# Two more head pairs take their V rows straight from memory, and the attention phase gets a new list

## The chip, the cores and the metric

The kernel runs on one core of a Trainium2 chip. The metric is the device time of one execution in microseconds (us). The core has a matmul engine (PE, whose weight loads are listed apart as PEld), a vector engine (DVE), an activation engine (ACT), a general engine (POOL), and SP, which here only issues DMAs. Each engine works through its own instructions in order; a semaphore makes one wait for another.

## The reference

Three stages follow one another. Attention over 2 batches of 8 heads (768 positions of 64 elements) sees, for each query, a band of keys (|distance| < 16) together with 24 block summaries (the block maximum of K, the block mean of V):

```
k_sum = k.reshape(B, H, nb, 32, D).max(axis=3)
v_sum = v.reshape(B, H, nb, 32, D).mean(axis=3)
scores_l = where(|i - j| < 16, scale * q @ k.T, -1e9)
scores_s = scale * q @ k_sum.T + log(32)
a = softmax(concat([scores_l, scores_s]))
attn = a @ concat([v, v_sum])
```

A token mixer and a channel mixer follow (`u = x + (relu(x.T @ w_tok1) @ w_tok2).T`, then `u + relu(u @ w_ch1) @ w_ch2`), and a second channel mixer behind a layer norm (2048 hidden columns). Everything is fp32.

## The kernel before

Two heads make a pair: 8 pairs, i = 0 to 7, four for each batch. A pair's 768 positions are cut into 12 windows of 64, and four windows make one quad, so there are 24 quads, n = 0 to 23, three to a pair. For one quad the attention phase does this, each step by a letter and a number:

- `q` (PE): scores, 8 small matmuls; `m` (DVE): mask, scale and row minimum; `e` (ACT): exponential into `pr`; `t` (PE): four transposes of `pr`; `c` (ACT): copy of them to `PT`; `a` (PE): product with V, tile `av`; `n` (DVE): division by the row sums into `u`.
- For each pair: `l` loads K and Q, `k` (DVE) forms the block maxima, `K` (ACT) or `J` (POOL) copies them beside the keys.

V reaches its tile `V[i % 3]` (rows are keys, columns are the two heads' elements) in one of two ways. For pairs i < `NT` (4 before), `v` loads a transposed V with a border (tile `VW`, 552 KB); `s` (DVE) or `p` (POOL) sums its blocks, `S` (ACT) or `T` (POOL) writes their means into it, `w` (PE, L446) transposes four windows per call, and `x` (ACT) or `X` (DVE) copies the result out of PSUM (L453). That is three `w` and three copies for a pair. For pairs i >= `NT`, `r` loads the finished rows into `V` (780 KB, L354), `v` loads a transposed V without borders (tile `VT`, 384 KB) for the means alone, `s` (POOL, L400 and L403) folds its blocks in halves, `S` (PE, L426) transposes the sums (tile `psv`), `z` (ACT, L430) scales them, and `u` (POOL, L438) copies them to the V rows.

Between the quads stand pieces of the token mixer: `g` starts piece k on PE, `G` and `H` copy its result out (ACT and DVE). Pieces 0 to 3, 10, 11, 20 and 21 are its first product (L575, tile `g`), 4 to 9 its second for batch 0 (L317 to L319), 12 to 19 transposes of `u` (L620). `h`, `W`, `D`, `C` and `O` load, unpack and split weights; `f` is a filler matmul on a tile of zeros (L1194).

The order is written out by hand: the string `FRONT` is walked from left to right, and each engine gets its instructions in that order. Nothing is moved later. A wait in one entry so holds up all that stands behind it on the same engine, and on SP all loads behind it. When the list is through, the channel mixer begins with the first matmul of `g_('u', 0)_3`; from there on no list is involved.

PSUM tiles of `w` and of the mixer's pieces come from a pool of two banks (`ps_mm`); the filler has a tile of the same pool. `t` and `psv` share two banks of `ps_pt`. `P` starts a transposing piece in a bank of `ps_pt`.

Of the kernel before, what the change touches and what calls it, by code (L numbers as in the profile page):

```python
# [11 lines left out]
F32 = mybir.dt.float32  # L12
# [3 lines left out]
AF = mybir.ActivationFunctionType  # L16
# [13 lines left out]
NK = 96 + NB  # L30
# [14 lines left out]
EARLY = 16  # L45
NEG = -8e9
EPS = 1e-9
NT = 4
FRONT = """
d0 f d1 f j0 f f j1 f f i0 v0 f i1 f l1 f K0 f v1 q0 l2 f f m0 f f e0 f h1 q1 t0 m1 f c0 f q2  # L50
e1 f m2 f l3 e2 t1 s0 f f f v2 t2 k1 S0 h2 w1 v3 w0 K1 x1 h0 q3 X0 c1 w2 m3 p1 a0 e3 q4 n0 c2 t3 m4
x2 a1 e4 k2 q5 T1 a2 n1 K2 c3 w3 m5 W1 t4 x3 D1 q6 c4 a3 e5 n2 w5 m6 w4 x5 t5 x4 n3 q7 p2 c5 k3 a4
e6 m7 a5 e7 t6 n4 r4 q8 n5 J3 S2 p3 t7 c6 m8 h4 w7 W2 y2 w6 X7 c7 q9 l4 e8 X6 a7 D2 v4 a6 S3 W0 v5
n7 w11 l5 w9 m9 x11 t8 x9 w8 D0 c8 q10 x8 w10 n6 e9 g1 X10 W4 k4 D4 K4 s4 t9 m10 C4 g0 c9 O4 G1 e10
H1 s5 q11 G0 H0 t10 l6 m11 S4 a8 e11 k5 q12 h3 z4 t11 c10 h7 n8 u4 a9 h5 m12 v7 e12 a10 n9 r5 J5 q13
n10 c11 t12 m13 a11 c12 k6 e13 q14 S5 a12 J6 m14 z5 e14 u5 t13 n12 q15 n11 c13 t14 W3 m15 a13 W7 D3
q16 e15 g2 m16 e16 s7 n13 D7 C3 c14 t15 O3 C7 q17 c15 t16 m17 G2 a14 e17 H2 q18 n14 r7 c16 a15 m18
e18 a16 l7 n15 q19 n16 W5 g3 h6 D5 v6 h8 m19 C5 h9 e19 r6 O5 t17 t18 G3 c17 q20 H3 k7 c18 g7 m20 K7
e20 g5 H7 W6 q21 H5 s6 g8 m21 e21 D6 S7 g6 W8 H8 h10 C6 D8 z7 t19 W9 u7 S6 g4 z6 O6 h11 H6 u6 q22 H4
g9 m22 e22 q23 H9 a18 m23 b g19 n18 g12 G19 a17 G12 H19 t20 H12 c19 g13 n17 c20 g16 t21 G16 a19 G13  # L60
H16 e23 a20 H13 n19 g11 c21 n20 t23 G11 g15 H11 t22 G15 g14 c22 H15 a21 G14 g18 c23 n21 a22 G18 H14
a23 n22 g10 n23 H18 g20 G10 H10 g21 G20 H20 P17 G21 G17 H21 H17
"""
SCALE = 1.0 / math.sqrt(D)

# [1 line left out]
def f32(ap):  # L67
    return ap.bitcast(F32)


class Kern:
# [342 lines left out]
    def prep_v2(self, i):  # L414
        nc = self.nc
        if i < NT:
            zs = self.vs.pop(i)
            nc.scalar.activation(
                self.wide[i][:, :, 0:NB],
                zs.rearrange("p (o n) -> p o n", o=1).to_broadcast([P, 7, NB]),  # L420
                AF.Copy,
                scale=1.0 / BLOCK,
            )
            return
        self.psv = self.ps_pt.tile([P, 512], F32, tag="pt", name=f"psv{i}")
        nc.tensor.transpose(self.psv[:NK, 0:P], self.Z[i % 2], self.ident)  # L426

    def prep_v3(self, i):
        self.zs = self.att.tile([NK, P], F32, tag="zs", bufs=1, name=f"zs{i}")
        self.nc.scalar.activation(self.zs, self.psv[:NK, 0:P], AF.Copy, scale=1.0 / BLOCK)  # L430

    def prep_v4(self, i):
        nc, src = self.nc, self.zs
        V = self.V[i % 3].rearrange("p (w j) c -> p j w c", j=2)
        for a, j in ((0, 0), (96, 1)):
            out = V[a : a + NB, j, :, 0:130].rearrange("p w (r c) -> p w r c", r=2)[:, :, :, 0:64]
            x = src[a : a + NB].rearrange("p (o r c) -> p o r c", o=1, r=2).to_broadcast([NB, 6, 2, 64])
            nc.gpsimd.tensor_copy(out, x)  # L438

    def att_vtr(self, n):  # L440
        i, qd = divmod(n, 3)
        ps = self.ps_mm.tile([P, 512], F32, tag="mm", name=f"vtr{n}")
        for u in range(4):
            w = 4 * qd + u
            a = 184 * (w // 2) + 88 * (w % 2)
            self.nc.tensor.transpose(ps[:NK, u * P : u * P + P], self.flat_vt(i)[:, a : a + NK], self.ident)  # L446
        self.vps[n] = ps
# [748 lines left out]
    def run(self):  # L1196
        tc, nc, ctx = self.tc, self.nc, self.ctx
# [38 lines left out]
        self.vs, self.vps, self.sn = {}, {}, {}  # L1236
# [220 lines left out]
```

## Time and profile before

| | |
|---|---|
| time, median of 3 runs | 558.04 us (557.51 to 558.55) |
| the profiled execution | 557.49 us, of which the trace's span is 555.7 us |
| PE busy over the span | 548.7 us (99%) |
| PEld busy | 495.0 us (89%) |
| DVE, ACT, POOL busy | 405.1, 272.2, 36.6 us |
| attention phase (start to the first matmul of the channel mixer) | 0 to 91.28 us |
| the rest | 91.28 to 555.7 us |

A PE row's duration runs from a matmul's start to its modelled end and overlaps the next one; how long PE is taken by an operation is read from the distance between starts. POOL works only in the attention phase.

### The profile page before, as it was taken

The page shows a single profiled execution, that of the slowest core. Times are in us where ns is not written, and L with a number is a line of the kernel's source. Part 1 is how long each engine was busy: PE and PEld are TensorE (multiplying, and loading weights), DVE is VectorE, ACT ScalarE, POOL GpSimd, SP SyncE. Part 2 cuts the span into 40 slices and gives each one's busy share as a digit, 9 for nine tenths or more (in the row PEclk, how much of TensorE's full clock was granted, in tenths as well). Part 3 has the DMA queues.
Part 4 walks back from the last instruction along what each step waited for, and adds up shares of the span by engine and source line. Part 5 has one row for each costly group of instructions (what it writes and reads, how often), then busy time and mean ns, then how long its engine had stood idle before and what let it go on. Part 6 is the DMA issues. An engine that isn't in the chain of part 4 may idle for free.

```text
span 555.7 us, 10285 instructions
## 1 busy us (share of the span) xinstructions
PE 548.7 (99%) x3673; PEld 495.0 (89%) x3674; DVE 405.1 (73%) x977; ACT 272.2 (49%) x602; POOL 36.6 (7%) x76
## 2 busy tenths in 40 slices
PE   8999999999999999999999999999999999999997
PEld 4887789898998989989999988988989999999997
DVE  5989874648876887665579957888866776777771
ACT  5979663138755645454787325554422222334320
POOL 7454400000000000000000000000000000000000
PEclk9999999999999999999999999999999999999999
DMA  8876810435788779888656996898787897777455
GB/s 326 313 298 242 327 57 1 151 109 197 248 297 292 266 282 315 283 313 296 230 207 234 317 312 195 284 313 278 257 300 234 292 314 253 240 234 254 162 168 173
DMA packets 55651, 137.00 MB, mean 247 GB/s; under 512 B 5681, under 2 KB 13489, under 8 KB 55601
## 3 DMA queue, kind: packets, MB, share of 16 engines
q1 hardware_dynamic: 55600, 136.36, 71.6%
q8 instruction: 29, 0.48, 0.3%
q14 instruction: 22, 0.17, 0.1%
HBM read 101.73 MB, written 34.60 MB: 245 GB/s over the span
## 4 chain that ended last, share of the span: by engine, by line
PE 91%; ACT 3%; DVE 2%; DMA 2%; POOL 0%; issue 0%; SPq 0%; DVEq 0%; POOLq 0%; ACTq 0%
PE m L319 8%; PE m L318 8%; PE m L317 8%; PE acc_x L318 4%; PE acc_x L319 4%; PE acc_x L317 4%; PE g L575 3%; PE acc_y L319 2%; PE acc_y L318 2%; PE acc_y L317 2%; DMA V<-in_v_dram 2%; ACT pr L519 1%; PE av L547 1%; PE acc_m L319 1%; PE acc_m L318 1%; PE acc_m L317 1%
## 5 line engine op out<-in xcount | busy, mean ns | idle before, releaser
L317 PE MATMUL m<-slot,slot 128*128 128x384 f32 (+1 forms) x136 | 45.8, 337 | 0.0
L319 PE MATMUL m<-slot,slot 128*128 128x384 f32 (+1 forms) x136 | 45.4, 334 | 0.0
L318 PE MATMUL m<-slot,slot 128*128 128x384 f32 (+1 forms) x136 | 45.4, 334 | 0.0
L319 PE MATMUL acc_x<-slot,al 128*128 128x512 f32 x96 | 37.8, 394 | 0.0
L318 PE MATMUL acc_x<-slot,ah 128*128 128x512 f32 x96 | 37.8, 394 | 0.0
L317 PE MATMUL acc_x<-slot,ah 128*128 128x512 f32 x96 | 37.5, 391 | 0.0
L519 ACT ACTIVATE pr<-sn,mn 128x120 f32<-128x120 f32 x96 | 29.7, 389 | 6.6 <-DVE mn L504 6.6
L317 PEld LDWEIGHTS m<-slot,slot 128*128 128x128 f32 x136 | 25.6, 188 | 1.8
L318 PEld LDWEIGHTS m<-slot,slot 128*128 128x128 f32 x136 | 25.6, 188 | 1.6
L165 DVE SCALAR_TENSOR_TENSOR dec<-stage,dec 128x512 uint32<-128x512 uint32 x36 | 25.5, 708 | 0.7
L319 PEld LDWEIGHTS m<-slot,slot 128*128 128x128 f32 x136 | 25.5, 188 | 0.0
L142 ACT ACTIVATE dec<-stage 128x512 f32<-128x512 f32 x36 | 24.2, 676 | 0.1
L871 ACT ACTIVATE ah<-sm 128x384 fp32r<-128x384 f32 x16 | 8.4, 525 | 28.1 <-DVE sm L881 28.1
L575 PE MATMUL g<-u,tok 128*128 128x256 f32 x96 | 22.1, 383 | 0.0
L504 DVE CUSTOM_DVE_ANT_0 sn<-scores,mask 128x120 f32<-128x120 f32 x92 | 20.4, 277 | 2.2 <-PE scores L485 2.1
L703 ACT ACTIVATE f_B<-tx,gt 128x384 f32<-128x384 f32 x16 | 9.3, 582 | 25.4 <-PE tx L699 25.4
L319 PEld LDWEIGHTS acc_x<-slot,al 128*128 128x128 f32 x96 | 18.0, 188 | 4.0
L243 DVE TENSOR_TENSOR slot<-dec,slot 128x512 fp32r<-128x512 f32 x27 | 20.1, 743 | 0.1
L319 PE MATMUL acc_y<-slot,al_s 128*128 128x256 f32 x72 | 20.1, 280 | 0.0
L318 PE MATMUL acc_y<-slot,ah_s 128*128 128x256 f32 x72 | 20.1, 279 | 0.0
L575 PEld LDWEIGHTS g<-u,tok 128*128 128x128 f32 x96 | 17.8, 190 | 2.6 <-issue 0.3
L666 ACT ACTIVATE xn<-u,nb,rs 128x128 f32<-128x128 f32 x48 | 20.1, 483 | 0.0
(1516 smaller groups left out, 1732.5 us busy)
## 6 DMA issues: line engine op xcount, KB each, us to landing
stage<-in_wts_dram SPq DMA_DIRECT2D x62, 512.0 KB, 4.4
slot<-w1s SPq DMA_DIRECT2D x94, 256.0 KB, 3.6
w1s<-sps SPq DMA_DIRECT2D x16, 512.0 KB, 4.4
w2s<-sp SPq DMA_DIRECT2D x16, 512.0 KB, 3.4
slot<-w2s SPq DMA_DIRECT2D x16, 512.0 KB, 4.8
w2t<-wk SPq DMA_DIRECT2D x16, 512.0 KB, 5.0
slot<-w2t SPq DMA_DIRECT2D x8, 768.0 KB, 5.0
slot<-w2s SPq DMA_DIRECT2D x22, 256.0 KB, 4.3
```

The lines of the kernel that those rows point to most:

```text
L142: fold = lambda out: nc.scalar.activation(out, high, AF.Prelu, scale=2.0**-112, alpha=-(2.0**32))
L165: put(m, t[:, :, 0], 29, m, op0=ALU.logical_shift_right, op1=ALU.bitwise_or)
L243: (engine or nc.vector).tensor_tensor(wl, x, f32(wh), op=ALU.subtract)
L317: nc.tensor.matmul(out, lhs[0], rhs[0], start=first, stop=False)
L318: nc.tensor.matmul(out, lhs[0], rhs[1], start=False, stop=False)
L319: nc.tensor.matmul(out, lhs[1], rhs[0], start=False, stop=last)
L504: nc.vector.tensor_tensor_reduce(sn[:, u], ps[u % 2][:, u // 2, :NK], self.mask[:, mv], scale=-SCALE, scalar=3e38, op0=ALU.add, op1=ALU.mi ...
L519: self.nc.scalar.activation(self.pr[n][:, u], sn[:, u], AF.Exp, bias=mn[:, u : u + 1], scale=-1.0)
L575: nc.tensor.matmul(ps[:, :256], self.tok1(st, t), self.u[:, b * ST + st, 256 * hf : 256 * hf + 256], start=st == 0, stop=st == ST - 1,)
L666: nc.scalar.activation(xn[:, j], self.u[:, g * GT + j, cc * P : cc * P + P], AF.Identity, bias=nb[:, j : j + 1], scale=rs[:, j : j + 1],)
L703: nc.scalar.activation(x, ps[:, :GN], AF.Copy, scale=self.gt[:, cc : cc + 1])
L871: nc.scalar.activation(ah, x, AF.Relu)
```

## The change

`NT` falls from 4 to 2: pairs 2 and 3 take the way of pairs 4 to 7. The tiles that hold a pair's sums between `S`, `z` and `u` are kept by pair, so that two pairs can be under way at once. Two banks of `ps_mm` are taken as fixed tiles at the start, and a helper hands them out in turn; the filler writes to the first of them. `FRONT` is a new list. It has 16 fillers instead of 22, 6 `w` instead of 12, and 6 copies behind them instead of 12.

```diff
-NT = 4
+NT = 2
 FRONT = """
-d0 f d1 f j0 f f j1 f f i0 v0 f i1 f l1 f K0 f v1 q0 l2 f f m0 f f e0 f h1 q1 t0 m1 f c0 f q2
+d0 d1 f f j0 f j1 f v0 f l1 f i0 f v1 f i1 l2 f f K0 q0 v2 f h2 m0 q1 e0 f m1 f f e1 q2 t0 s0 l3 f
...
+    def mm_bank(self, name):
+        if not self.banks:
+            return self.ps_mm.tile([P, 512], F32, tag="mm", name=name)
+        self.banks.rotate(1)
+        return self.banks[0]
...
-        self.psv = self.ps_pt.tile([P, 512], F32, tag="pt", name=f"psv{i}")
-        nc.tensor.transpose(self.psv[:NK, 0:P], self.Z[i % 2], self.ident)
+        self.psv[i] = self.ps_pt.tile([P, 512], F32, tag="pt", name=f"psv{i}")
+        nc.tensor.transpose(self.psv[i][:NK, 0:P], self.Z[i % 2], self.ident)
...
     def att_vtr(self, n):
         i, qd = divmod(n, 3)
-        ps = self.ps_mm.tile([P, 512], F32, tag="mm", name=f"vtr{n}")
+        ps = self.mm_bank(f"vtr{n}")
...
     def g1(self, b, hf, t):
         nc = self.nc
-        ps = self.ps_mm.tile([P, 512], F32, tag="mm", name=f"g1_{b}_{hf}_{t}")
+        ps = self.mm_bank(f"g1_{b}_{hf}_{t}")
...
-            ps = self.bank or self.ps_mm.tile([P, 512], F32, tag="mm", name=f"tu_{g}_{cc}")
+            ps = self.bank or self.mm_bank(f"tu_{g}_{cc}")
...
-        self.wps = self.ps_mm.tile([P, 512], F32, tag="mm", name="warm_ps")
+        self.banks = deque(self.ps_mm.tile([P, 512], F32, tag="mm", name=f"mm{i}") for i in range(2))
+        self.wps = self.banks[0]
...
         with tc.manual_schedule(engines={E.PE}):
             self.attention()
+        self.banks = None
```

Counted over the two lists: `f` 22 to 16, `w` 12 to 6, `x` 8 to 4, `X` 4 to 2, `p` 3 to 1, `s` 5 to 7, `T` 1 to 2, `r` 4 to 6, `z` and `u` 4 to 6 each, `K` 5 to 7 and `J` 3 to 1; three splits of weights go from DVE (`O`) to POOL (`o`); three more transposing pieces stand in `ps_pt` banks (`P` 1 to 4). `S` falls from 7 to 6: of pairs 0 to 3 it had been an ACT copy for 0, 2 and 3, and is now a PE transpose for 2 and 3. All else in the list occurs as often as before. From the first matmul of the channel mixer on, the instructions of PE are the same in both programs.

PE, behind the third score product, up to the first transposes of V. Before:

```order
L485 MATMUL scores<-K_135,Q_132 64x120 x8
L1194 LDWEIGHTS warm
L1194 MATMUL warm_ps<-warm 128x512
...
L528 MATMUL pt_299<-ident,pr_279 120x128 x4
L1194 LDWEIGHTS warm
L1194 MATMUL warm_ps<-warm 128x512
...
L528 MATMUL pt_310<-ident,pr_294 120x128 x4
L446 MATMUL vtr_320<-ident,VW_109 120x128 x4
```

and now (line numbers are 6 higher from here on):

```order
L491 MATMUL scores<-K_133,Q_130 64x120 x8
L534 MATMUL pt_272<-ident,pr_245 120x128 x4
L1200 LDWEIGHTS warm
L1200 MATMUL mm_187<-warm 128x512
...
L534 MATMUL pt_284<-ident,pr_259 120x128 x4
L452 MATMUL mm_188<-ident,VW_109 120x128 x4
```

Behind the third score product there were two groups of transposes and five fillers before the first `vtr`, with one more group ahead of it; now there are two groups and two fillers in all. `mm_187` and `mm_188` are the two fixed banks.

PE, from the last transposes of probabilities before pair 2's V up to the first mixer piece. `VW_111` and `VW_112` are the transposed V of pairs 2 and 3. Before:

```order
L528 MATMUL pt_593<-ident,pr_559 120x128 x4
L446 MATMUL vtr_607<-ident,VW_111 120x128 x4
L446 MATMUL vtr_614<-ident,VW_111 120x128 x4
L485 MATMUL scores<-K_135,Q_132 64x120 x8
L547 MATMUL av_637<-V_142,PT_139 64x65 x8
L547 MATMUL av_649<-V_142,PT_138 64x65 x8
L446 MATMUL vtr_664<-ident,VW_112 120x128 x4
L446 MATMUL vtr_671<-ident,VW_112 120x128 x4
L528 MATMUL pt_683<-ident,pr_631 120x128 x4
L446 MATMUL vtr_689<-ident,VW_111 120x128 x4
L485 MATMUL scores<-K_135,Q_132 64x120 x8
L446 MATMUL vtr_706<-ident,VW_112 120x128 x4
```

and now:

```order
L432 MATMUL psv_553<-ident,Z_143 120x128
L534 MATMUL pt_555<-ident,pr_482 120x128 x4
L491 MATMUL scores<-K_133,Q_130 64x120 x8
L534 MATMUL pt_582<-ident,pr_540 120x128 x4
L553 MATMUL av_595<-V_139,PT_137 64x65 x8
L491 MATMUL scores<-K_133,Q_130 64x120 x8
L553 MATMUL av_625<-V_140,PT_136 64x65 x8
L534 MATMUL pt_639<-ident,pr_604 120x128 x4
L553 MATMUL av_655<-V_140,PT_137 64x65 x8
L491 MATMUL scores<-K_133,Q_130 64x120 x8
L534 MATMUL pt_677<-ident,pr_650 120x128 x4
L581 MATMUL mm_188<-u,tok 128x256 x6
```

Six groups of four transposes are gone, and one transpose of a pair's sums (`psv`) stands for three of them.

POOL, behind its work for pair 1. Before (`vh` are the halves of pairs 2 and 3, `VT_143` is the first pair that folds):

```order
L406 TENSOR_SCALAR VW_110<-vs_356 128x7x24
L376 TENSOR_TENSOR vh_521<-VW_111 128x384
...
L373 COPY K_135<-ks_528 128x7x24
L376 TENSOR_TENSOR vh_587<-VW_112 128x384
...
L376 TENSOR_TENSOR vs_586<-vh_587 128x24
L400 TENSOR_TENSOR VT_143<-VT_143 128x24x16
```

and now (`V_140` and `V_138` are the V tiles of pairs 2 and 3):

```order
L412 TENSOR_SCALAR VW_110<-vs_344 128x7x24
L406 TENSOR_TENSOR VT_141<-VT_141 128x24x16
...
L409 TENSOR_TENSOR Z_143<-VT_141 128x24 x2
L444 COPY V_140<-zs_574 24x6x2x64 x2
L406 TENSOR_TENSOR VT_142<-VT_142 128x24x16
...
L409 TENSOR_TENSOR Z_144<-VT_142 128x24 x2
L444 COPY V_138<-zs_733 24x6x2x64 x2
L243 TENSOR_TENSOR slot_103<-dec_674,slot_103 128x512
```

POOL now does the sums and the row copies of pairs 2 and 3 in turn, and a split of weights behind them.

## Rows read from the trace of the kernel before

**Rows 1.** Stretches: length, then busy time by engine, granted clock, DMA share, GB/s.

```profile
core 0: us, PE busy (x) PEld busy (x) DVE busy (x) ACT busy (x) POOL busy (x), PEclk, DMA share, GB/s
...
5.40:11.76 6.36, 6.22 (x72) 3.62 (x73) 4.00 (x26) 4.47 (x14) 3.94 (x6) 1.00 1.01 401
11.76:30.59 18.83, 18.60 (x329) 15.31 (x330) 17.30 (x84) 17.85 (x49) 8.61 (x20) 1.00 0.88 334
30.59:76.67 46.08, 44.05 (x571) 34.81 (x569) 41.90 (x173) 34.21 (x97) 19.69 (x34) 1.00 0.68 255
...
91.28:555.70 464.42, 461.18 (x2583) 427.17 (x2581) 333.82 (x674) 209.24 (x431) 0.00 (x0) 1.00 0.74 248
```

**Rows 2.** Waits of PE from 0 to 91.3 us: total, times, longest.

```profile
...
PE g L317 <- DVE u L604: 0.9, 1, 0.9
PE scores L485 <- POOL V L438: 0.5, 1, 0.5
PE scores L485 <- DVE mn L504: 0.4, 1, 0.4
```

**Rows 3.** Timeline of PE: start, duration, line, operation, count.

```profile
1.25 4.07 PE L1194 MATMUL warm_ps<-warm 128*128 128x512 bf16 x10 [1.25 <-DVE warm L1247]
...
5.98 1.25 PE L1194 MATMUL warm_ps<-warm 128*128 128x512 bf16 x5
...
10.37 0.81 PE L1194 MATMUL warm_ps<-warm 128*128 128x512 bf16 x3
11.02 0.66 PE L528 MATMUL pt<-ident,pr 128*120 128x128 f32 x4
11.76 1.09 PE L446 MATMUL vtr<-ident,VW 128*120 128x128 f32 x8
12.78 0.64 PE L485 MATMUL scores<-K,Q 64*64 64x120 f32 x16
...
39.59 1.15 PE L547 MATMUL av<-V,PT 121*64 121x65 f32 x32
...
43.01 0.33 PE L426 MATMUL psv<-ident,Z 128*120 128x128 f32 x1
43.27 0.69 PE L547 MATMUL av<-V,PT 121*64 121x65 f32 x16
...
91.28 0.42 PE L317 MATMUL g_('u', 0)_3_1578<-xt,slot 128*128 128x384 f32 x1
```

**Rows 4.** Groups of ACT up to 91.5 us: count, busy, mean ns, idle before.

```profile
...
L453 ACT COPY V<-vtr 120x512 f32<-120x512 f32 x8 | 4.5, 589 | 0.2 <-PE vtr L446 0.2
...
L373 ACT COPY K<-ks 128x168 f32<-128x168 f32 x5 | 1.7, 331 | 3.5 <-DVE ks L364 3.5
...
L430 ACT ACTIVATE zs<-psv 120x128 f32<-120x128 f32 x4 | 1.1, 264 | 1.6 <-POOL V L438 1.6
L418 ACT ACTIVATE VW<-vs 128x168 f32<-128x168 f32 x3 | 1.0, 338 | 0.1
```

**Rows 5.** Timeline of POOL.

```profile
19.78 1.02 POOL L376 TENSOR_TENSOR vh<-VW 128x384 f32<-128x384 f32 x1 [4.00 <-DMA VW<-in_vk_dram]
...
33.71 2.82 POOL L400 TENSOR_TENSOR VT<-VT 128x384 f32<-128x384 f32 x4 [7.90 <-DMA VT<-in_vt_dram]
...
49.73 2.47 POOL L438 COPY V<-zs 24x768 f32<-24x768 f32 x2 [6.04 <-DMA V<-in_v_dram]
...
65.86 2.06 POOL L438 COPY V<-zs 24x768 f32<-24x768 f32 x2 [0.27 <-ACT zs L430]
```

**Rows 6.** Timeline of DVE: one split beside POOL's work, one without.

```profile
34.12 1.14 DVE L243 TENSOR_TENSOR slot<-dec,slot 128x512 fp32r<-128x512 f32 x1
...
57.16 0.69 DVE L243 TENSOR_TENSOR slot<-dec,slot 128x512 fp32r<-128x512 f32 x1
```

**Rows 7.** Timeline of SP: the load of a weight half.

```profile
23.67 0.38 SPq L210 DMA_DIRECT2D stage<-in_wts_dram  x1
```

**Rows 8.** Tile V up to 95 us: times from issue to landing.

```profile
DMA to landing us min/median/max: 4.1/7.0/9.7
```

More of the change, by code (lines that the diff above doesn't have):

```diff
@@ L47 @@
 EPS = 1e-9
-NT = 4
+NT = 2
 FRONT = """
-d0 f d1 f j0 f f j1 f f i0 v0 f i1 f l1 f K0 f v1 q0 l2 f f m0 f f e0 f h1 q1 t0 m1 f c0 f q2
[L51 to L59, printed above, removed]
@@ L60 @@
-g9 m22 e22 q23 H9 a18 m23 b g19 n18 g12 G19 a17 G12 H19 t20 H12 c19 g13 n17 c20 g16 t21 G16 a19 G13
-H16 e23 a20 H13 n19 g11 c21 n20 t23 G11 g15 H11 t22 G15 g14 c22 H15 a21 G14 g18 c23 n21 a22 G18 H14
-a23 n22 g10 n23 H18 g20 G10 H10 g21 G20 H20 P17 G21 G17 H21 H17
+d0 d1 f f j0 f j1 f v0 f l1 f i0 f v1 f i1 l2 f f K0 q0 v2 f h2 m0 q1 e0 f m1 f f e1 q2 t0 s0 l3 f
+c0 f t1 m2 r2 e2 T0 h1 k1 w0 v3 w1 h0 K1 x0 q3 X1 c1 a0 m3 p1 e3 w2 n0 q4 x2 t2 m4 a1 e4 k2 q5 T1 t3
+m5 K2 s2 w3 c2 w5 e5 n1 q6 X5 a2 x3 m6 c3 t5 W2 n2 w4 e6 q7 k3 a3 m7 x4 t4 K3 D2 q8 c4 c5 a4 e7 m8
@@ new lines @@
+h4 S2 t6 r3 n4 q9 l4 z2 c6 u2 n3 t7 W1 m9 v4 a5 e8 D1 q10 s3 a6 c7 n5 W0 t8 m10 e9 a7 D0 q11 W4 v5
+t9 c8 h5 D4 g0 e10 l5 n6 h3 C4 m11 r4 e11 l6 n7 S3 g1 k4 z3 h7 G0 u3 H0 K4 c9 o4 q12 a8 m12 s5 a9
+e12 r5 n8 t11 t10 n9 G1 c11 q13 c10 a11 m13 s4 a10 e13 n11 q14 n10 W5 t12 t13 m14 g2 c13 H1 v6 c12
+k5 v7 l7 D5 K5 W3 S4 D3 C5 q15 h6 z4 g3 G2 u4 m15 e14 H2 C3 k6 o3 q16 G3 e15 a13 m16 o5 a12 e16 H3
+q17 n12 t14 m17 W7 S5 g8 c14 D7 K6 z5 e17 u5 t16 n13 t15 H8 g5 c15 s6 q18 a14 m18 a15 c16 r7 q19 n15
@@ L63 @@
+r6 s7 t17 h8 H5 g7 h9 c17 m19 e18 k7 g6 H7 S7 S6 H6 z7 q20 u7 t18 m20 g4 e20 n14 J7 z6 g9 e19 u6 W6
+q21 H9 a17 m21 a16 e21 H4 q22 c18 t19 m22 b g13 c19 t20 n17 W8 q23 n16 C7 a19 G13 D6 a18 g11 c20 H13
+h10 e22 m23 y2 n18 e23 n19 t21 G11 g15 c21 t22 H11 D8 G15 a20 C6 a21 c22 H15 h11 t23 n21 g14 c23 P16
+n20 a23 G16 G14 a22 n23 P12 n22 g10 G12 O6 W9 H12 H16 H14 P18 G10 g17 H10 P19 G17 g20 G19 H17 G18
+H18 g21 G20 H20 G21 H21 H19
 """
@@ L424, in prep_v2 @@
             return
-        self.psv = self.ps_pt.tile([P, 512], F32, tag="pt", name=f"psv{i}")
-        nc.tensor.transpose(self.psv[:NK, 0:P], self.Z[i % 2], self.ident)
+        self.psv[i] = self.ps_pt.tile([P, 512], F32, tag="pt", name=f"psv{i}")
+        nc.tensor.transpose(self.psv[i][:NK, 0:P], self.Z[i % 2], self.ident)
     def prep_v3(self, i):
-        self.zs = self.att.tile([NK, P], F32, tag="zs", bufs=1, name=f"zs{i}")
-        self.nc.scalar.activation(self.zs, self.psv[:NK, 0:P], AF.Copy, scale=1.0 / BLOCK)
+        self.zs[i] = self.att.tile([NK, P], F32, tag="zs", bufs=1, name=f"zs{i}")
+        self.nc.scalar.activation(self.zs[i], self.psv.pop(i)[:NK, 0:P], AF.Copy, scale=1.0 / BLOCK)
     def prep_v4(self, i):
-        nc, src = self.nc, self.zs
+        nc, src = self.nc, self.zs.pop(i)
         V = self.V[i % 3].rearrange("p (w j) c -> p j w c", j=2)
@@ L592, in g2 @@
         for st in range(ST) if only is None else (only,):
-            ps = self.ps_mm.tile([P, 512], F32, tag="mm", name=f"g2_{b}_{st}")
+            ps = self.mm_bank(f"g2_{b}_{st}")
             for t in range(2):
@@ L1235, in run @@
         self.VT = [att.tile([P, S], F32, name=f"VT{i}") for i in range(2)]
-        self.vs, self.vps, self.sn = {}, {}, {}
+        self.vs, self.vps, self.sn, self.psv, self.zs = {}, {}, {}, {}, {}
         self.Z = [att.tile([P, NK], F32, name=f"Z{i}") for i in range(2)]
```

## Prediction

> **What bounds the kernel now.** I first split the span at 91.28 us, where the channel mixer starts [rows 3]. Behind it PE works 461.18 of 464.42 us [rows 1], and the change leaves PE's instructions there as they are. So this part is carried along by whatever moves its start, and only the attention phase is open. A gain there is a gain in the total, unless a wait takes it.
>
> In the attention phase I read the stretches by engine next. From 11.76 to 30.59 us PE is busy 18.60 of 18.83 us, ACT 17.85 and DVE 17.30; from 30.59 to 76.67 us PE 44.05 of 46.08, DVE 41.90, ACT 34.21 [rows 1]. Nothing has much room before 30 us; later ACT has. Then I asked what PE waits for: the waits above 0.3 us, behind the first matmul, come to 0.9 + 0.5 + 0.4 = 1.8 us [rows 2]. A busy PE row may still hide a wait, since its end is modelled. So I take PE's costs from the distance between starts in the timeline [rows 3]: eight transposes of V take 12.78 - 11.76 = 1.02 us, 0.128 us each, and the next operation follows at once. Reading: PE sets the pace of the phase, with ACT and DVE close behind until 30 us.
>
> By the Trainium skill, page "Trainium Kernel Development and Optimization", section "Performance Expectations", busy matmul time says little about how full PE is, and the busy share of weight loads says more. PEld is at 15.31 of 18.83 us before 30.59 us [rows 1], so by that rule a fifth of this stretch is not PE's own, and work taken from PE there need not come back in full; this is the second rival below.
>
> **The change, part by part.** All in us on PE's path unless said otherwise.
>
> 1. *Six groups of four V transposes go* (pairs 2 and 3). 24 x 0.128 = 3.1. I take -3.0, since groups with other work on both sides come out a little shorter. Bounds: nothing, if PE waits for something else at these places; and -3.3, with a tenth more for the switch between shapes.
>
> 2. *Two transposes of block sums come.* One takes 43.27 - 43.01 = 0.26 [rows 3]: with 0.2 each, as it costs less between other 128-row transposes, +0.4. Bounds +0.2 to +0.6.
>
> 3. *Six fillers go.* Three take 11.02 - 10.37 = 0.65, so 0.22 each [rows 3], 1.3 for six. All stand in the first 12 us, where PE waits for the chain of scores, minimum and exponential: if this chain is no earlier, PE waits where it had filled, and the gain is 0. But the new list also puts the second quad's minimum and exponential straight behind the first's, where a copy out of PSUM had stood between them, and it starts V's transposes behind two groups of probabilities instead of three. So I take the full -1.3. Bounds 0 to -1.8.
>
> 4. *ACT.* Four copies out of PSUM (589 ns) and three of means (338 ns) go, two `zs` (264 ns) and two K copies (331 ns) come [rows 4]: -2.4 - 1.0 + 0.5 + 0.7 = -2.2 of ACT's time. DVE loses two copies and three splits, 0.69 to 1.14 each [rows 6]. Both are freed by about half as much as PE or more, so neither is made the bound by work of its own. On the path: 0.
>
> 5. *POOL.* For each of the two pairs it folds a transposed V (2.82 up to the last fold) and copies V's rows (2.06) [rows 5]; two halvings of the old way go. The three splits have 512 columns; the nearest row, a tensor-tensor of 384 columns, took 1.02, so by width 1.4 each is my estimate; 1.0 and 2.7 (twice it) are its ends. POOL was busy 8.61 of 18.83 and 19.69 of 46.08 us [rows 1]. With 2 x 4.9 + 4.2 = 14 more it stays at two thirds. Its throughput is covered; its latency is the rival below.
>
> What this does to DVE shows in one pair of rows: the split at 34.12, while POOL was folding from 33.71 to 36.53, took 1.14, and the same at 57.16, with POOL at rest, 0.69 [rows 5, 6]. The Trainium skill, page "SBUF — State Buffer", section "Who interferes with whom", gives the reason: a DVE instruction with two SBUF inputs and a POOL instruction that reads SBUF exclude each other for a whole instruction; this trace agrees in kind (0.45 us lost, not the whole fold). If all of the 4.2 us of splits on POOL were to block DVE, it would lose 0.8 more than the largest 3.4 that it sheds by them, and DVE has 46.08 - 41.90 = 4.2 of idle time in that stretch [rows 1]: 0 on the path, by rule and by row.
>
> 6. *Loads.* A transposed V and the rows are 384 + 780 KB instead of 552 KB: 1224 KB more for both pairs, 1.25 MB, at the 401 GB/s of the first stretch [rows 1] 3.1 us of transfers. The DMA share is 0.68 from 30.59 to 76.67 us, some 14 us free, so the sum fits; single loads may come up to 3.1 later. The load of pair 3's rows now stands on SP behind a weight load that before was issued at 23.67 [rows 7], because it waits for DVE to empty its buffer. From there, 4.1 to 9.7 us to landing [rows 8] and a copy of 2.06 make its V ready at 29.8 to 35.5, at the median 32.7. PE reached the corresponding product (the first of pair 3, tenth of 24) at 39.59 [rows 3]. Between 11.76 and there the new list has six V groups less (-3.0), two groups of probabilities less up to that product (-1.3; one group lasts 0.66 [rows 3]), one block-sum transpose more (+0.2), and the fillers' -1.3: 34.2. At the median landing this is no wait; at the longest it is 1.3. I take 0, with 0 to +1.3 for each such pair.
>
> 7. *Two fixed banks in turn* replace a pool of two banks that is handed out in turn as well: 0. The fillers share a bank with the first transposes, but all on PE, in order: 0. Three more pieces in `ps_pt` banks stand near the end of the list, with few probability groups left to share them: 0, up to +0.5 each (the old wait for POOL, [rows 2]) for a bank not yet read.
>
> 8. *The old waits* of 1.8 us [rows 2] stand at places that the new list rearranges. I let them stay as a sum. Bounds -1.8 (gone) to the rivals below.
>
> Sum: -3.0 + 0.4 - 1.3 = -3.9. The profiled execution took 557.49 us (span 555.7 and 1.8 around it); it would take 553.6. The median of the three runs is 0.55 higher, 558.04; the same step from there gives 554.1, which is the forecast. The first matmul of the channel mixer should stand at about 87.4.
>
> **Rivals.**
>
> *More than the sum.* The old waits go too: -3.9 - 1.8 = -5.7, 552.3. For it: all engines but POOL get less to do. Against: a new list has its own places to wait.
>
> *ACT sets the pace up to 30 us.* It is busy 95% there [rows 1]. Then the phase gains what ACT is freed of, -2.2, and not PE's 3.9: 555.8. Against: the V transposes at 11.76 follow each other at 0.128 and leave no pause behind them [rows 3], and none of the waits in [rows 2] is for ACT.
>
> *One wait for V takes the gain; or the clock does.* If the loads are slower by the added 3.1, pair 3's V comes at 23.67 + 9.7 + 3.1 + 2.06 = 38.5, a wait of 4.3 at 34.2, and the total is 558.04 - 3.9 + 4.3 = 558.4: no change. The same comes out if, with fewer fillers, the granted clock stays low: the first ten matmuls ran at 0.41 each, three later ones at 0.22 [rows 3], the two levels of 1.2 and 2.4 GHz, and 4 us of work at half speed would cost 4. Against: the ten fillers ahead of the first scores stay.
>
> *Slower: V's rows late for two pairs in a row.* POOL works in order, so a late V for pair 3 holds its folding for pairs 4 and 5, and its row copies for pair 4 stand behind that and a split. If the wait of 4.3 comes twice, the sum is -3.9 + 8.6 = +4.7: 562.7. The trace has the pattern: POOL sat 6.04 us waiting for V's load before 49.73 [rows 5], and PE then waited 0.5 for POOL [rows 2]. It decides from two waits of 2.5 on (5.0 in all, 3.9 and the 1.1 below): for pair 3, when its V is ready after 36.7. Against: that 6.04 cost PE only 0.5, and pair 2's load goes into a tile that nothing has used yet.
>
> *The change doesn't do what it says* is excluded by the order: six V groups are gone from PE.
>
> **How the numbers follow.** Forecast 554.1 with chance 0.48 (its own range 552.9 to 555.3, from the bounds of parts 1 to 3). More than the sum, 552.3: 0.10. ACT's pace, 555.8: 0.17. One wait or the clock, 558.4: 0.12. Two waits, 562.7: 0.13. About 0.2%, or 1.1 us, is what a measurement of this kernel can tell from no change; faster then means below 556.9. The first three are faster, 0.75; the fourth is the same, 0.12; the last is slower, 0.13. The range leaves out the two-wait case and the edges of the others: 551.8 to 558.5.
>
> **What would show it.** Right: the channel mixer's first matmul between 86 and 89 us and a remainder of 464.4 us behind it; 24 V transposes instead of 48; the first V transposes at 10 to 11 us; no PE wait above 1 us for POOL's row copies. Step 3 is wrong if PE idles between the first scores and the first V transposes for as long as the fillers took. Part 4 is wrong if ACT is busy over 95% from 12 to 30 us again and PE's pauses end with it. The forecast as a whole is wrong if PE waits for POOL's V copy of pairs 2 to 5 for more than 2 us in sum, or if the stretch behind the phase isn't 464.4 us.

## The result and the profile after

The changed kernel takes 552.20 us (551.81 to 552.57, 4 runs) beside 557.77 us of the kernel before: a ratio of 0.9898 [0.9881, 0.9916], 5.6 us less. The forecast was 554.1, with 551.8 to 558.5 as its range. It is faster as forecast, but by the size of the first rival, "more than the sum" (552.3, given a chance of 0.10); it lies below the forecast's own range of 552.9 to 555.3.

| | before | after |
|---|---|---|
| the profiled execution, its span | 557.49, 555.7 | 551.81, 550.0 |
| first matmul of the channel mixer | 91.28 | 85.47 |
| from there to the end of the span | 464.42 | 464.53 |
| first transposes of V | 11.76 | 9.75 |
| from there to the channel mixer | 79.52 | 75.72 |
| PE's listed idle time up to the channel mixer | 2.03 | 1.34 |
| POOL busy over the span | 36.6 | 42.2 |

All of the gain is made ahead of the channel mixer, 2.01 us up to the first transposes of V and 3.80 behind them (5.81); the rest is carried along. The stretches of after that answer to [rows 1], in the same columns:

```profile
9.75:29.15 19.40, 18.11 (x331) 14.13 (x329) 18.10 (x90) 18.86 (x55) 11.21 (x20) 1.00 1.00 397
29.15:60.00 30.85, 30.80 (x385) 24.96 (x384) 23.85 (x110) 21.18 (x61) 19.98 (x35) 1.00 0.82 317
...
85.47:550.00 464.53, 461.33 (x2582) 427.28 (x2580) 333.39 (x674) 208.60 (x430) 0.00 (x0) 1.00 0.75 248
```

Up to 29.15 us three engines are near full at once: ACT 18.86 of 19.40 us, PE 18.11, DVE 18.10. From 29.15 to 60 us PE alone is full (30.80 of 30.85). The waits of PE up to 86 us, which answer to [rows 2]:

```profile
PE mm L1200 <- DVE warm L1253: 1.2, 1, 1.2
PE av L553 <- ACT pr L525: 0.9, 1, 0.9
PE scores L491 <- ACT K L379: 0.2, 1, 0.2
PE mm L581 <- DVE hl L593: 0.2, 1, 0.2
```

No wait is for POOL, so none for V's rows. The three old waits of 1.8 us in sum are gone; a new one of 0.9 has come. PE's timeline at the places that answer to [rows 3]:

```profile
8.37 0.65 PE L534 MATMUL pt<-ident,pr 128*120 128x128 f32 x4
9.08 0.38 PE L1200 MATMUL mm<-warm 128*128 128x512 bf16 x1
9.29 0.60 PE L534 MATMUL pt<-ident,pr 128*120 128x128 f32 x4
9.75 1.09 PE L452 MATMUL mm<-ident,VW 128*120 128x128 f32 x8
...
27.37 0.69 PE L553 MATMUL av<-V,PT 121*64 121x65 f32 x16 [0.94 <-ACT pr L525]
...
85.47 0.53 PE L317 MATMUL g_('u', 0)_3_1518<-xt,slot 128*128 128x384 f32 x1
```

To see where the 5.81 us lie, I took PE's time from start to start in both timelines, less the listed idle times, and summed it by kind of work up to the channel mixer. This counts a hidden wait to the work ahead of it.

| PE's time up to the channel mixer, us | before | after | change | predicted |
|---|---|---|---|---|
| transposes of V (48, 24) | 5.99 | 3.21 | -2.78 | -3.0 |
| transposes of block sums (4, 6) | 0.55 | 0.86 | +0.31 | +0.4 |
| fillers (22, 16) | 6.73 | 5.62 | -1.11 | -1.3 |
| listed idle time | 2.03 | 1.34 | -0.69 | 0 |
| transposes of probabilities (96 in each) | 13.15 | 12.20 | -0.95 | 0 |
| all other work, the same in both | | | -0.6 | 0 |

The three terms of the sum are there, each a little smaller, with two that it did not have. But this table only says where time stood. What a term is worth by itself was to be tested.

### The profile page after: what moved, and what is told of

The parts are those of the page before. It is cut to its first block, busy times and chain, and to the rows that moved or that the text cites. A ratio compares the mean times of both kernels' runs of the same rounds, so it can differ in the third digit from the quotient of the medians.

```text
span 550.0 us, 10236 instructions
## 1 busy us (share of the span) xinstructions
PE 543.9 (99%) x3645; PEld 491.7 (89%) x3646; DVE 399.5 (73%) x972; ACT 270.1 (49%) x599; POOL 42.2 (8%) x81
## 4 chain that ended last, share of the span: by engine, by line
PE 93%; ACT 2%; DVE 2%; POOL 1%; issue 1%; POOLq 0%; DVEq 0%; ACTq 0%
PE m L319 8%; PE m L318 8%; PE m L317 8%; PE acc_x L318 4%; PE acc_x L319 4%; PE acc_x L317 4%; PE mm L581 3%; PE acc_y L319 2%; PE acc_y L318 2%; PE acc_y L317 2%; PE scores L491 1%; PE pt L534 1%; ACT pr L525 1%; PE av L553 1%; PE acc_m L319 1%; PE acc_m L317 1%
## 5 line engine op out<-in xcount | busy, mean ns | idle before, releaser
L165 DVE SCALAR_TENSOR_TENSOR dec<-stage,dec 128x512 uint32<-128x512 uint32 x36 | 24.8, 690 | 0.7
L581 PE MATMUL mm<-u,tok 128*128 128x256 f32 x96 | 22.2, 383 | 0.2 <-DVE hl L593 0.2
L169 DVE SCALAR_TENSOR_TENSOR dec<-stage,dec 128x512 uint32<-128x512 uint32 x23 | 15.9, 690 | 7.3 <-ACT stage L142 6.7
L581 PEld LDWEIGHTS mm<-u,tok 128*128 128x128 f32 x96 | 17.7, 190 | 2.9 <-DVE hl L593 0.4
```

Source lines behind the costliest of these rows:

```text
L165: put(m, t[:, :, 0], 29, m, op0=ALU.logical_shift_right, op1=ALU.bitwise_or)
L169: put(m, t[:, :, 1], 3, m, op0=ALU.logical_shift_left, op1=ALU.bitwise_or)
L581: nc.tensor.matmul(ps[:, :256], self.tok1(st, t), self.u[:, b * ST + st, 256 * hf : 256 * hf + 256], start=st == 0, stop=st == ST - 1,)
```

## The experiments

The theories behind them: (A) PE paces the phase, so that work taken from PE comes back in full; (B) ACT and DVE pace it, as full as PE is; (C) the supply of V (loads, POOL's folds) paces it. Each ratio is to the kernel before, measured beside it.

**Less work in the old list.** The first kernel is the old list without the six V transposes of pairs 2 and 3 and the copies behind them; the second keeps the transposes and drops the copies alone.

```diff
 the list of the kernel before
-w6 w7 w8 w9 w10 w11
-x8 X6 X7 x9 X10 x11
 zeros where no copy writes
-nc.gpsimd.memset(t[96 : NK + 1], 0.0)
+nc.gpsimd.memset(t[96 : NK + 1] if t is not self.V[2] else t[0 : NK + 1], 0.0)
```

> The kernel before without the six V transpose groups of pairs 2 and 3 and without the six copies behind them (their V rows are not formed: pair 2's tile holds zeros, pair 3's keeps pair 0's rows). Theory A (PE's own list sets the pace, each of its groups gives back its start-to-start time): 24 transposes at 0.12 to 0.13 us, channel mixer starts 2.8 to 3.1 us earlier than 91.3, total about 554.9 against 557.8. Theory B (the gain of the changed kernel comes from its new order and shorter waits; V's transposes were hidden beside ACT and DVE): under 1 us.

> The kernel before without the six copies out of PSUM behind the V transposes of pairs 2 and 3 alone (four on ACT, two on DVE; V rows of these pairs are not formed); the transposes stay. Theory A: ACT and DVE are freed, PE is not: 0 to 0.4 us. Theory B (ACT and DVE pace the stretch from 12 to 31 us): ACT's 2.0 us come back, total about 555.8.

Measured: 558.57 (557.24 to 560.85), 1.002 [1.0002, 1.0039] without both, and 558.53 (557.60 to 559.49), 1.0009 [0.9999, 1.002] without the copies. Neither gains. (Three of the ten executions of the first, 560.56 to 560.85 us, had a mean granted clock of 0.997, the others 0.999 or 1.00; the median of these seven is 557.65, still no gain.) In the first, PE's time for V transposes fell by 2.97 us and its listed idle time rose from 2.03 to 4.97. PE's waits there, in the columns of [rows 2], and then the stretch from 11.76 us:

```profile
PE scores L485 <- DVE mn L504: 1.9, 4, 0.7
...
PE scores L485 <- POOL VT L400: 1.2, 1, 1.2
PE psv L426 <- POOL Z L403: 0.8, 1, 0.8
PE scores L485 <- POOL vh L376: 0.7, 1, 0.7
PE g L575 <- DVE tok L165: 0.4, 1, 0.4
```

```profile
11.76:30.59 18.83, 16.55 (x308) 13.00 (x307) 17.27 (x82) 17.80 (x50) 8.64 (x20) 1.00 0.83 314
```

PE has fallen from 18.60 [rows 1] to 16.55 us of this stretch. ACT (17.80) and DVE (17.27) are as full as before, though the copies are gone. So A falls for the old list: the PE work that leaves is replaced by waits, all of them for DVE or POOL. B falls as far as it is about ACT, with the second kernel: there ACT is busy 16.64 us of the same stretch, 1.2 less than before, and the 2.0 us that B promised don't come back. DVE is as full there as before (17.19).

**The supply of V.** The two loads of transposed V for pairs 4 and 5 are moved up, without the V transposes and with them.

```diff
 the list without w6 to w11 and their copies; in a second kernel the whole old list
-... D2 v4 a6 S3 W0 v5 ...
+... x1 h0 v4 v5 q3 ...
```

> e1 once more (the list of before without the six V transpose groups and their copies; V rows of pairs 2 and 3 not formed), with the loads of the transposed V of pairs 4 and 5 moved ahead on SP, to before the load of pair 4's V rows that had held them from 13 to 26 us. Theory C (in the list of before a chain of SP, DMA and POOL, from the load of pair 4's V rows over the folds to pair 5's rows, ends as late as PE does, and held e1 up): POOL's 7.8 us wait for the transposed V goes, PE's waits for POOL in e1 (0.7, 0.8, 1.2 us) mostly go, and the channel mixer starts 1.5 to 3 us earlier than in e1: 89 to 90.5, total 555 to 556.5. Theory D (e1 was held by DVE and ACT alone, the waits for POOL are only the last of several): within 0.5 us of e1.

> The kernel before with only those two loads moved ahead on SP; nothing removed. Theory C: PE's own list is as long as the chain, so 0 to 0.7 us (at most its 0.5 us wait for POOL goes). Theory D: 0.

Measured: 558.11 (556.78 to 559.82), 1.0006 [0.9996, 1.0017], and 558.93 (558.36 to 561.50), 1.0027 [1.0016, 1.0038]. The second is even 1.5 us slower; PE has a wait of 0.8 us there, for DVE's division, that it did not have before, and I did not follow its cause further. POOL's wait of 7.8 us for those loads is gone in the first, yet the channel mixer starts at 91.90 us (92.11 with the loads where they were). PE's timeline there shows what is late instead:

```profile
25.59 0.64 PE L485 MATMUL scores<-K,Q 64*64 64x120 f32 x16 [0.59 <-DVE mn L504]
...
29.16 0.64 PE L485 MATMUL scores<-K,Q 64*64 64x120 f32 x16 [1.02 <-DVE mn L504]
...
30.22 2.86 PE L575 MATMUL g<-u,tok 128*128 128x256 f32 x12 [0.42 <-DVE tok L165]
...
53.59 0.64 PE L485 MATMUL scores<-K,Q 64*64 64x120 f32 x16 [1.18 <-POOL VT L400]
```

and POOL's timeline what stands behind the last of them:

```profile
49.70 2.44 POOL L438 COPY V<-zs 24x768 f32<-24x768 f32 x2 [5.76 <-DMA V<-in_v_dram]
52.21 2.81 POOL L400 TENSOR_TENSOR VT<-VT 128x384 f32<-128x384 f32 x4
```

C falls as the only cause as well. Up to 38 us DVE's row minimum is late (B), then pair 5's rows: their tile is that of pair 2, whose last product starts at 37.30 us; their load is issued at 39.71, behind six other loads on SP, and the copy starts at 49.70. When one cause is taken away, the next holds PE at nearly the same time.

**The two halves of the change apart.** One kernel has direct rows for pairs 2 and 3 in the old list, each entry put where the corresponding old one stood; the other has the new list and the fixed banks, but V of pairs 2 and 3 by transposes.

```diff
 direct rows, old list
-NT = 4
+NT = 2
-p2 p3, w6 to w11 and their copies
+s2 for p2; c6 z2 u2 s3 for c6; v3 r2 for v3; r3 r4 for r4; c8 z3 u3 for c8
 V by transposes, new list
-NT = 2
+NT = 4
-r2 r3 z2 u2 z3 u3 s2 s3
+p2 p3, w6 to w11 and their copies x6 X7 x8 x9 X10 x11, at S2, W1 and D4
```

> One part alone: V rows of pairs 2 and 3 loaded directly, in the order of before (their V transposes and copies are gone, the folds, the transposes of sums and the row copies stand where the old sums and copies stood; all else as before). Theory A (PE's work alone): -3.0 + 0.4, total about 555. Theory E (in the order of before PE, DVE and SP's loads of V end together from 12 to 54 us, so that work taken from PE alone turns into waits, as in e1): 0 to 1 us faster, or slower by up to 3 where pair 3's rows come late; the gain of 5.6 us needs the new order.

> The other part alone: the new order and the fixed banks, but V of pairs 2 and 3 over transposes as before (six transpose groups and six copies back, halvings on POOL, no early loads of their rows). If both parts are needed: 2 to 4 us of the 5.6 are lost, total 554.5 to 556.5, the channel mixer starts at 88 to 89.5. If the order alone does it: under 1 us lost. If the direct rows alone do it: all is lost, 557.8.

Measured: direct rows in the old list 561.84 (561.13 to 562.90), 1.0063 [1.0046, 1.0081]; transposes in the new list 556.63 (556.40 to 557.24), 0.9979 [0.997, 0.9989]. So one half is 4.2 us slower, the other 1.0 faster, and both together 5.6 faster. The gain belongs to neither half as it was run. Each was run in one placement of its entries only, so that 4.2 and 1.0 need not be what a half is worth in its best one. What the direct rows do in the old list, from PE's timeline and then by stretches:

```profile
31.81 0.47 PE L426 MATMUL psv<-ident,Z 128*120 128x128 f32 x1 [2.82 <-POOL Z L403]
32.07 1.06 PE L528 MATMUL pt<-ident,pr 128*120 128x128 f32 x4
...
38.29 0.60 PE L528 MATMUL pt<-ident,pr 128*120 128x128 f32 x4
```

```profile
31.80:34.00 2.20, 2.19 (x21) 1.62 (x21) 0.75 (x1) 0.83 (x3) 0.01 (x1) 0.50 0.88 270
34.00:36.00 2.00, 2.00 (x9) 1.57 (x6) 0.34 (x1) 1.85 (x6) 1.86 (x3) 0.50 1.02 406
36.00:38.00 2.00, 2.00 (x8) 1.66 (x7) 1.97 (x7) 0.47 (x1) 1.86 (x2) 0.70 0.44 176
38.00:40.00 2.00, 2.00 (x13) 1.77 (x12) 1.13 (x6) 1.22 (x5) 1.82 (x5) 1.00 0.00 0
```

PE waits 2.82 us for POOL's sums of pair 3, whose fold began at 27.87 behind pair 2's row copy. The placement has its part in this: where the old list had an ACT copy of means, a PE transpose now stands, and PE asks for the sums at 28.99, 2.8 us before they are there. The same list with this entry further back was not run. Behind this pause the granted clock is 0.50 (the level of 1.2 GHz) until about 37 us; four transposes take 1.06 us there and 0.60 after it. By my estimate from the rows' clocks the stretch loses 2.20 x 0.50 + 2.00 x 0.50 + 2.00 x 0.30 = 2.7 us. With the pause that is 5.5 us, of the size of the phase's loss (the channel mixer starts at 96.77, 5.5 later than before). But the removed transposes and this list's other waits are in that loss too, and how much the clock alone costs was not run. The profiled execution is the slowest of the four: two took 562.49 and 562.90 us at a mean clock of 0.994, the other two 561.13 and 561.19 at 0.997. The 1.5 us between the pairs are near what 0.003 of the clock makes over the span (an estimate: 1.7 us).

In the other kernel the gain of 1.0 is made at the start: the first transposes of V stand at 10.29 us, 1.47 earlier than before, and from there to the channel mixer it takes 80.02 us, 0.5 more. The new list has its own waits where the transposes of pairs 2 and 3 stand, for ACT's copies of block means:

```profile
23.78 1.09 PE L452 MATMUL mm<-ident,VW 128*120 128x128 f32 x8 [1.18 <-ACT VW L424]
31.99 1.09 PE L452 MATMUL mm<-ident,VW 128*120 128x128 f32 x8 [0.94 <-ACT VW L424]
```

So in the new list the old way of V costs 80.02 - 75.72 = 4.30 us behind the first V transposes. These two waits are 2.12 of it; the next experiment finds 1.72 for the PE work alone, and the rest was not taken apart.

**The PE work put back into the new kernel.** Six groups of four V transposes on data already there, each behind a score product. They overwrite some of pair 1's transposes before those are copied, so two of its groups of V rows are altered.

```diff
+    def dummy_vtr(self, n):
+        ps = self.mm_bank(f"dummy{n}")
+        for u in range(4):
+            self.nc.tensor.transpose(ps[:NK, u * P : u * P + P], self.flat_vt(n % 2)[:, 88 * u : 88 * u + NK], self.ident)
...
-q6 ... q11
+q6 Y0 ... q11 Y5
```

> The changed kernel with six more groups of four V transposes on PE, one behind each of the score products 6 to 11, written to the two banks and read by nobody (extra work). Theory A: channel mixer starts 2.8 to 3.1 us later than 85.5, total 555.0 to 555.3. Theory B: PE has waits there that take them up, under 1 us later.

Measured: 553.99 (553.35 to 554.20), 0.9928 [0.9911, 0.9944]. The groups take 3.30 us of PE. The channel mixer starts at 87.80, 2.33 later; but 0.61 of that lies ahead of the first V transposes (10.36 us), where nothing was added. From there on it is 77.44 - 75.72 = 1.72 us, which the times repeat: 0.9928 - 0.9898 = 0.0030, or 1.7 us. In three kernels further down that keep the new list and its work on PE from there on (without the last fillers, with banks from the pool, with one decode moved) the same stretch takes 75.67 to 75.82 us, so that 1.72 is clear of the spread. The first stretch there:

```profile
9.75:29.15 19.40, 19.13 (x317) 15.09 (x316) 17.09 (x88) 17.72 (x50) 10.09 (x18) 1.00 0.94 375
```

Now PE is full (19.13 of 19.40 us), and the 0.94 us wait has gone. PE's listed idle time fell by 0.91 us, and the transposes of probabilities behind the first V transposes by 0.30, which the table's counting takes for hidden waits: together most of what did not show. So in the new list V transposes on PE cost about half of their time (1.7 of 3.3); in the old list taking them out gave nothing.

**Fillers.** Six fewer in the old list, and the new list without its last six.

```diff
 before: six f behind the first ten left out
 after: every f behind the first ten left out
```

> The kernel before without six of its fillers (four of the five behind the first scores, the last two ahead of quad 2's transposes). Prediction's step 3: 1.3 us faster. If fillers only fill PE's waits for the chain of minimum and exponential: 0 within 0.3, the first V transposes still start at about 11.8.

> The changed kernel without the six fillers behind the first ten. If fillers only fill PE's waits: 0 within 0.2 us, the first V transposes start at 9.75 as before. If they stand on the path: 1.1 to 1.3 us earlier. If the clock falls with them: the first matmuls run at twice their time, up to 3 us later.

Measured: 557.74 (556.91 to 558.12), 0.9997 [0.9988, 1.0007] for the old list, and 552.22 (551.78 to 554.05), 0.9912 [0.9891, 0.9932] for the new one, which is the changed kernel's own time. Fillers are worth nothing in either median. In both profiled executions the granted clock is 1.00; but the one of 554.05 us had a mean of 0.997, so the clock rival isn't excluded for the new list. It can't be laid to the fillers either: 0.996 and 0.997 also came with all fillers in place (one execution in ten with the early loads, three in ten without V transposes). Why the first V transposes don't come earlier shows in the old list with six fewer. ACT's timeline, then PE's:

```profile
9.12 2.40 ACT L519 ACTIVATE pr<-sn,mn 128x120 f32<-128x120 f32 x8
11.58 0.34 ACT L418 ACTIVATE VW<-vs 128x168 f32<-128x168 f32 x1
```

```profile
10.80 1.09 PE L528 MATMUL pt<-ident,pr 128*120 128x128 f32 x4
11.98 1.09 PE L446 MATMUL vtr<-ident,VW 128*120 128x128 f32 x8
```

The transposes start 0.06 us after ACT has written the means into the transposed V. This is their gate, whatever PE does until then. Nothing of it is listed as a wait. The kernel before has the same gate; the means end at 11.70 us there, and the transposes start at 11.76:

```profile
11.36 0.34 ACT L418 ACTIVATE VW<-vs 128x168 f32<-128x168 f32 x1
```

In the changed kernel the entry `S0` (ACT) became `T0` (POOL), and DVE's block sums stand ahead of the third row minimum:

```profile
8.01 0.95 DVE L399 TENSOR_REDUCE vs<-VW 128x24 f32<-128x768 f32 x1
```

```profile
9.05 0.64 POOL L412 TENSOR_SCALAR VW<-vs 128x168 f32<-128x168 f32 x1 [0.92 <-DVE vs L399]
```

The sums end at 8.96, POOL's means at 9.69, and the transposes start at 9.75. Without its last six fillers the new list shows this gate as a listed wait:

```profile
9.82 1.09 PE L452 MATMUL mm<-ident,VW 128*120 128x128 f32 x8 [0.50 <-POOL VW L412]
```

**Fixed banks, and the one wait left.** Banks handed out by the pool in the new kernel; then the new list with one decode of weights behind the division of quad 5.

```diff
-self.banks = deque(self.ps_mm.tile(...) for i in range(2))
+self.banks = None
 in the other kernel
-e8 D1 q10 s3 a6 c7 n5
+e8 q10 s3 a6 c7 n5 D1
```

> The changed kernel with its products in tiles of the two-bank pool, as before, instead of two fixed banks. Theory A: same order of banks, same waits, 0 within 0.2 us. Rival: the pool makes a tile wait for more than its own bank, up to 2 us slower.

> The changed kernel with one entry moved: the unpacking of the second weight half on DVE (0.80 and 1.38 us there, beside POOL's folds) stands behind the division of quad 5 instead of ahead of it. PE's longest wait, 0.94 us before the product at 27.4, is put down to that division holding a bank. If so: the wait goes and the channel mixer starts 0.5 to 0.9 us earlier, at about 84.7, total 551.5. If ACT held it (as the waits' list names ACT): 0.

Measured: 552.08 (551.79 to 552.30), 0.9896 [0.9882, 0.9911] and 552.32 (551.71 to 552.68), 0.9901 [0.9887, 0.9916], both no change from the new kernel. The banks are worth 0. The wait of 0.94 us at 27.37 is gone in the second, and another is there, with the same 75.8 us from the first V transposes to the channel mixer:

```profile
28.78 0.64 PE L491 MATMUL scores<-K,Q 64*64 64x120 f32 x16 [1.17 <-DVE mn L510]
```

**Pair 1 by direct rows too.** A try for a faster version, with `NT = 1`.

```diff
-NT = 2
+NT = 1
-p1 w3 w4 w5 x3 x4 X5 T1
+s1 S1 z1 u1 r1, s2 moved behind u1
```

> A step further: pair 1's V rows loaded directly as well, in the changed kernel's order (three transpose groups, three copies and a mean less; a fold, a transpose of sums and a row copy more; 612 KB more in the first 17 us). If PE, DVE and ACT are relieved and the rows come in time: 0.5 to 1.3 us faster than 552.2. If the first loads are the bound, as the DMA queues are full there: pair 1's first product waits, 1 to 3 us slower.

Measured: 564.84 (563.57 to 565.71), 1.012 [1.0099, 1.014]. It decides nothing on its question: in my list pair 3's transposed V is loaded into pair 1's tile ahead of pair 1's fold, so the fold waited for that load and formed pair 1's means from pair 3's V. It shows the clock once more, though. From PE's timeline, and the stretch behind it:

```profile
27.68 0.47 PE L432 MATMUL psv<-ident,Z 128*120 128x128 f32 x1 [12.16 <-POOL Z L409]
```

```profile
27.60:30.00 2.40, 2.32 (x33) 1.79 (x33) 0.67 (x7) 1.82 (x7) 1.45 (x3) 0.50 0.00 0
```

None of these kernels beats the changed one.

## Why the prediction was right, step by step

- **The whole.** The direction was right, the total in part by luck. Of the sum's -3.9 us the runs bear out 1.7 for the V transposes and nothing for the fillers; 2.0 came from an earlier start for which the prediction had another reason, and 2.1 more behind it had no term in the sum. Of its signs the remainder behind the phase (464.53 us), the 24 V transposes and the missing waits for row copies hold; the channel mixer (85.47, said to be 86 to 89) and the first V transposes (9.75, said to be 10 to 11) came earlier than named. The own range of 552.9 to 555.3 doesn't follow from the bounds of parts 1 to 3 either: these add up to 553.1 to 558.6.
- **What bounds the kernel.** "PE sets the pace of the phase, with ACT and DVE close behind until 30 us" was half of it. The split at the channel mixer held to 0.1 us. But "close behind" was binding: taken from the old list, PE's 2.97 us came back as 2.94 us of waits. The rule of the Trainium skill that was set against the row (page "Trainium Kernel Development and Optimization", section "Performance Expectations": busy matmul time says little) is borne out here. PE's busy 18.60 of 18.83 us looked like a bound; without the transposes it was 16.55 in the same stretch, and the phase was no shorter.
- **Step 1, -3.0.** In the table -2.78. Its bound "nothing, if PE waits for something else at these places" was the truth in the old list. In the new list half of the put-back work shows, so about 1.7 us of the total is its own.
- **Step 2, +0.4.** +0.31.
- **Step 3, -1.3.** Its sum is near (-1.11), its reason wrong. Six fillers are worth 0 in both lists. The start moved from 11.76 to 9.75 us since the block sums and their means are made earlier and not by ACT, which I had not looked at: I read the gate off PE's row alone. In all kernels with the old list the first V transposes stand at 11.76 to 12.54 us, with the new one at 9.75 to 10.36 (9.45 in the last one, with pair 1 by direct rows, aside): some 2 us, with as many fillers or fewer. The move of the sums was not run by itself.
- **Step 4, 0.** The copies alone are worth 0 in the old list, as said. But by the prediction's own test ("ACT is busy over 95% from 12 to 30 us again and PE's pauses end with it") it fails in this stretch: ACT is busy 17.26 of 18.00 us, and the one pause is put down to ACT's exponential. I don't read that pause as ACT's, see step 5. The rival "ACT's pace" priced ACT at its own -2.2; the phase gained 5.8, so ACT alone does not set it.
- **Step 5, 0.** POOL's throughput is covered, and a split of 512 columns took 1.27 us (estimate 1.4). What did not hold is that POOL costs DVE nothing on the path. DVE's timeline, a decode without POOL's work and one beside POOL's row copy (23.26 to 24.97) and fold (25.06 to 27.93):

```profile
20.67 0.42 DVE L160 TENSOR_SCALAR tok<-tok 128x512 uint32<-128x512 uint32 x1
21.13 0.69 DVE L165 SCALAR_TENSOR_TENSOR tok<-stage,tok 128x512 uint32<-128x512 uint32 x1
...
24.46 0.80 DVE L160 TENSOR_SCALAR tok<-tok 128x512 uint32<-128x512 uint32 x1
25.29 1.38 DVE L165 SCALAR_TENSOR_TENSOR tok<-stage,tok 128x512 uint32<-128x512 uint32 x1
26.60 0.17 DVE L567 RECIPROCAL rec<-av 128x4 f32<-128x4 f32 x1
26.80 0.42 DVE L570 TENSOR_TENSOR u<-av,rec 128x256 f32<-128x256 f32 x1
```

```profile
23.26 1.71 POOL L444 COPY V<-zs 24x768 f32<-24x768 f32 x2 [5.12 <-ACT zs L436]
25.06 2.87 POOL L406 TENSOR_TENSOR VT<-VT 128x384 f32<-128x384 f32 x4
```

  The two instructions lose 0.38 + 0.69 = 1.07 us. Behind them stands the division that empties the product's bank; it ends at 27.22, and PE's product, 0.94 late, starts at 27.37. With the decode behind the division that wait is gone, which fits, though ACT's part of the decode moves with it. By the order of work I take DVE as the one that was late, and the row's name of ACT as that of the semaphore that came last. The 0.94 could not be won by moving, since the next minimum was then late by 1.17.
- **Step 6, 0.** No PE wait for V's rows. The landing is longer than in [rows 8], as foreseen; this is tile V up to 95 us:

```profile
DMA to landing us min/median/max: 4.8/7.7/10.9
```

  The slow rival is not a fancy: the same direct rows in the old list bring a late pair 3 (2.82 us), and the clock with it, though it is pair 3's sums that are late and not its rows. It named two waits of 4.3 us; one wait and the clock behind it went with +4.2 us. The new list doesn't ask for pair 3's rows earlier (22.32 us, 18.36 in the old list). But it loads pair 2's transposed V at 6.43 us (10.96) and starts its fold at 15.17 (19.27), so that pair 3's sums end at 29.18 (31.75), and PE asks for them later, at 31.85 (28.99).
- **Step 7, 0.** Confirmed for the banks (552.08 us without them); no listed wait stands at the pieces in `ps_pt`.
- **Step 8, 0.** This is the mis-sized term. The old waits did go (-0.69 of listed idle time). A term that the sum lacked went with them, the transposes of probabilities at -0.95. Of it, 0.3 are hidden waits ahead of the first V transposes: the first three groups took 0.71, 0.61 and 0.74 us from start to start, now 0.71, 0.46 and 0.58. The rest goes with what follows a group in the new list: ahead of other transposes or the mixer's matmuls it takes 0.39 to 0.49 us, ahead of scores or products mostly 0.51 to 0.58. That is read from the rows, not tested by itself; that the term comes with the list shows in the kernel with the new list and V by transposes, where these groups take 12.37 us (12.20 in the changed one, 13.15 before). With -0.6 in other work these are 2.2, less 0.3 by which the first three terms came out smaller: the 1.9 us by which the phase beat the sum.

Open: what the move of the block sums, and what the half clock, cost by themselves; whether less DVE work between 10 and 29 us would help (the three splits back on DVE was not run); direct rows in the old list with pair 3's entries further back; and pair 1 by direct rows.

## What to carry to other kernels

Where three engines are each over 90% busy in a stretch, a saving on one is worth what the other two leave of it. Here it was nothing in the old list and half in the new one; so price it by asking which engine ends the next pause, and test the saving by itself. A change that comes with a new order should be split into its halves: here +4.2 and -1.0 us made -5.6 together. But a half needs its own placement, or its measured loss is that of one badly placed entry. And read the first instruction of a chain by its inputs, not by the row ahead of it: a filler that looks like cost may only fill a wait that the profile lists nowhere.

## What the runs showed of the hardware

- A pause of PE of 2.82 us, and one of 12.16 us, were each followed by a granted clock of 0.50 (1.2 GHz), in the first case for some 5 us; pauses of 0.94 and 1.18 us were followed by 1.00. Behind the 2.82 us the lost speed (2.7 us by the estimate above) costs about as much as the pause itself.
- The first score products run at different speeds from one execution to the next. At 5.56 us in the changed kernel 16 of them took 0.64 us; at 5.62, with the transposes put back, 1.08. With the decode moved they took 0.64 again, but only after a wait of 1.08 us for Q's load. That moves all that follows by some tenths, so that kernels of one list were compared from the first V transposes on:

```profile
5.62 1.08 PE L496 MATMUL scores<-K,Q 64*64 64x120 f32 x16
6.63 0.54 PE L1206 MATMUL mm<-warm 128*128 128x512 bf16 x1
7.11 0.64 PE L496 MATMUL sc<-K,Q 64*64 64x120 f32 x16
```

- POOL's row copy and its fold slowed DVE's instructions beside them to about twice their time (0.42 to 0.80, 0.69 to 1.38 us), one with a single tensor input among them. With the decode moved both stand beside the fold and take 1.13 and 0.97 us, again 1.0 more in all. It isn't so for every pair: the division at 26.80 us keeps its 0.42 beside the fold, and beside the next decode, from 27.95 us on, it is POOL that loses, 1.18 us for two sums that take 0.41 elsewhere. The Trainium skill, page "SBUF — State Buffer", section "Who interferes with whom", names both kinds, tensor-scalar for its two-port modes. It speaks of blocking for a whole instruction; the trace agrees if each of POOL's six instructions there counts apart, since DVE lost 1.07 us in all and not the 4.6 for which they ran.
